# Layer-norm roots by pairs of row tiles on ScalarE, sums ahead of statistics, and banks closed to early maxima ahead of transposes and products

## The chip, the cores and the metric

The kernel runs on one core of a Trainium2 chip. The core has five engines with queues of their own: TensorE (PE, matrix products into PSUM banks), VectorE (DVE), ScalarE (ACT), GpSimd (POOL) and SyncE (SP, which mostly issues DMA transfers). An engine executes its queue in the order in which the program was written, and waits at an instruction until the semaphores it needs are set. The metric is device microseconds of one execution; lower is better.

## The reference

Two kinds of layers alternate, twice each, on `x` of 2048 rows by 512 columns in float32:

```python
x = x + fnet(layernorm(x))     # Re(DFT over rows (DFT over columns))
x = x + attention(layernorm(x))
x = x + fnet(layernorm(x))
x = x + attention(layernorm(x))

def layernorm(x, eps=1e-5):
    m, v = mean(x), var(x)                  # of each row
    return (x - m) / sqrt(v + eps)

def attention(x):                           # 32 query heads of 16 columns, one key and value head
    q, k, v = heads(x @ wq), x @ wk, x @ wv
    p = softmax(q @ k.T * 16 ** -0.5)
    return merge(p @ v) @ wo
```

## The kernel before

The kernel calls the same code twice (`L` is 0 and 1), once for each pair of a Fourier layer and an attention layer. In each, phase A computes the Fourier layer, and, as rows come out of it, the layer norm, keys, values and queries of the attention; phase B computes the attention. In layer 0 phase A lasts from 0 to about 655 us and in layer 1 from about 1800 to 2440 us. The change touches phase A only.

Phase A goes through 128 steps `n`, 32 for each block `tb` of four row tiles of 128 rows. The steps multiply normalized rows with the sequence DFT matrix into four banks `z[d]`, as three products of high and low parts (`ch`, `cl` of the matrix, `xnh`, `xnl` of the rows). From step 48 on (`ROWS`) this is done by `z_rows` (L749) in pairs of 64-row matmuls for two steps at once. The banks of z are in the two pairs named `x` in PSUM. The second half of such a group waits for a relay (L542): ScalarE copies two elements of `xnl` onto themselves, which orders the halves.

When a block's steps are done, its y rows follow (`y_tile` for block 0, `y_rows`, L555, for blocks 1 and 2): the column DFT. `y_out` then, for each row tile, adds the residual (`x1`, L537) on VectorE, stores the sum to `mid` by a DMA from GpSimd, and takes the layer-norm statistics (`ln_stats`, L136 and L137, into `mv`). `prep_tasks` spreads the rest of the block's attention input over the next block's first steps. The table `ts` there maps (step within the block, z quarter done) to tasks; a key without a quarter is the end of that step:

- `ln_root(t0, 4)`: variance plus epsilon on VectorE (L142, `lnv`), its square root on ScalarE (L143, `lnw`), for all four tiles at once; `ln_inv`: a reciprocal on VectorE (L148) and one Newton round in four small GpSimd operations (L149 to L152), into `rs`.
- `ap(j)`: subtract the mean and multiply with the inverse root, on VectorE (`ln_apply`, L183).
- `tr(j)`: transpose a row tile by four matmuls with the identity (L258) into the single bank `z`, and split it into high and low parts (ScalarE L82, L83, GpSimd L84).
- `do_kv`: keys and values of the block, twelve matmuls (L87 to L89) into a bank `y`, of which there are three; `kv_lo` (L286) and `k_diff` (L296, L297, L300) read that bank on VectorE and ScalarE; `v_tr` (L305, L306) transposes the values through bank `z`.
- `q_mm`, four times: queries, each twelve matmuls into a bank `y`, then stores.

Into all this the kernel mixes "early maxima". Phase B needs the maximum of each query row's scores; the table `EARLY` lists those that phase A already computes, with the steps of load, start and deadline. One maximum is one score matmul (L440) into a free `y` or `z` bank and a reduce on VectorE (L454, into `mxp` or `mxe`); where keys come as differences (`kd`), ScalarE and a fused VectorE operation (L444, L449) do it in two parts. When and into which bank a maximum goes is fixed while the program is written, by a small clock model: `clk` holds an estimated time for TensorE, VectorE, ScalarE and each bank, `spend` and `held` advance it, `pump` places a maximum wherever the model says that a bank is free, and `flush(n)` places in a row whatever has passed its deadline at step `n`. The DFT matrix's splits for later steps (`c_split`: a cast on ScalarE, L78, and a difference on GpSimd, L79) come two steps ahead, for two steps at once.

Of the kernel before, what the change touches and what calls it, by code (L numbers as in the profile page):

```python
# [17 lines left out]
P = 128  # L18
# [8 lines left out]
EPS = 1e-5  # L27
# [20 lines left out]
def fnet_mqa_kernel(ctx: ExitStack, tc: tile.TileContext, x_in, ct, dt_, wq, wkv, wo, out):  # L48
# [48 lines left out]
    nc.gpsimd.memset(v1[:, :, DH:DH + 1], 1.0)  # L97
    kone = sb.tile([P, 1], F32, name="kone")
# [40 lines left out]
    def ln_root(t0, n):  # L139
        v = sb.tile([P, 4], F32, name="lnv", bufs=2)[:, :n]  # L140
        w = sb.tile([P, 4], F32, name="lnw", bufs=2)[:, :n]
        nc.vector.tensor_scalar(v, mv[:, t0:t0 + n, 1], EPS, None, op0=ALU.add)  # L142
        nc.scalar.activation(w, v, AF.Sqrt)  # L143
        return t0, n, v, w
# [43 lines left out]
    def make_layer(L, src, mid, dst, last):  # L188
# [75 lines left out]

        def kv(t0, n, xth, xtl, vt=None, now=True):
            pk = bank("y")[:, :n * P]
            spend(pe=2.9, act=1.2)
            held("y", clk["pe"] + 2.5)
# [39 lines left out]
        def q_mm(tb, g, xth, xtl):  # L308
            wh, wl = st["wqh", g]
            pq = bank("y")  # L310
            spend(pe=2.9, act=1.2)
            held("y", clk["act"])
# [100 lines left out]
        st["skew"], st["rel"] = 0, {}  # L413
# [9 lines left out]
        def issue(e, pr, part, g, force):  # L423
            i, kb = EARLY[e][:2]
            tag = "z" if clk["z"] <= clk["y"][0] else "y"
# [5 lines left out]
            if free > clk["pe"] + 0.05 and not force:  # L431
                return False
# [6 lines left out]
            pm = bank(tag)  # L439
            nc.tensor.matmul(pm, o.qT[i][gs, pr, :], k[gs, c0:c0 + 512], start=True, stop=True)  # L440
# [94 lines left out]
        def y_out(t, y, x1):  # L535
            spend(dve=1.3)
            nc.vector.tensor_add(x1, y, x1)  # L537
            nc.gpsimd.dma_start(mid[t], x1)
            ln_stats(x1, t)
# [4 lines left out]
        def y_rows(tb, pairs, zh, zl, x1, after):  # L544
            ys = [pair() for _ in pairs]
            at = 0
            for h in range(2):
                for w, y in zip(pairs, ys):
# [15 lines left out]
                    else:  # L564
                        for e in range(2):
                            y_out(4 * tb + w[e], y[:, e, :], x1[w[e]])
# [71 lines left out]
        def prep_tasks(tb, x1):  # L638
# [3 lines left out]
            def alloc():  # L642
                st["root"] = ln_root(4 * tb, 4)
# [13 lines left out]
            ts[0] = [alloc]  # L657
            ts[1, 1] = [lambda: ln_inv(*st["root"])]
            ts[2, 0], ts[2, 2] = [ap(0)], [ap(1)]
            ts[2] = [lambda: tr(0)]  # L660
            ts[3, 0], ts[3, 2] = [ap(2)], [ap(3)]
            ts[3] = [lambda: tr(1)]
            ts[4, 1] = [lambda: tr(2)]
# [527 lines left out]
```

## Time and profile before

| what | us |
|---|---|
| median of three runs (lowest, highest) | 3596.87 (3596.85, 3599.12) |
| the profiled execution | 3599.28 |
| span of its trace | 3597.4 |
| TensorE busy | 3513.1 |
| VectorE busy | 2685.1 |
| ScalarE busy | 2504.9 |
| GpSimd busy | 897.0 |

In the profile, a group is named by its line, engine and operation, and by out<-in in the program's tile names. Rows of the timeline give start, duration, engine, line, operation and tiles; in brackets stands how long the engine was idle just before, and which instruction ended that. Rows of the waits give the waiting line, the line waited for, the total, how often, and the longest. Rows of windows give for each stretch its length, the busy times and instruction counts of PE, PEld (weight loads), DVE, ACT and POOL, then TensorE's granted clock (1.00 is full), the DMA share and GB/s. The y rows of block 1 end at about 282 us in layer 0, and those of block 2 at about 460; in layer 1 the same places are at about 2064 and 2242.

### The profile page before, as it was taken

What the parts mean: (1) busy time and instruction counts of PE and PEld (TensorE: products, weight loads), DVE (VectorE), ACT (ScalarE), POOL (GpSimd) and SP (SyncE); (2) the same over time, 40 slices, a digit from 0 to 9 for tenths busy, and PEclk for the clock granted to TensorE, in tenths of its full rate; (3) what the DMA queues carried; (4) which work ended last, traced back from release to release, by engine and by line L of the source; (5) the groups of instructions that cost most, each with busy time, mean ns of one, the idle gap of its engine ahead of it and who ended that gap; (6) DMA issues with size and microseconds to landing.
All of it is one profiled execution on the core that took longest, in us unless ns stands there. A gap on an engine that the chain in (4) does not pass through costs nothing.

```text
span 3597.4 us, 64452 instructions
## 1 busy us (share of the span) xinstructions
PE 3513.1 (98%) x24672; PEld 1891.4 (53%) x24672; DVE 2685.1 (75%) x4853; ACT 2504.9 (70%) x3204; POOL 897.0 (25%) x1284
## 2 busy tenths in 40 slices
PE   8999999899999999999999999999999999999999
PEld 6797878433333333333378878783333333333333
DVE  6166776788888888888511777758888888888883
ACT  3322734688888888888933237437888888888888
POOL 5543332221122112212254342422010110011011
PEclk9999999999999999999999999999999999999999
DMA  6544252311111101110143342422111111111110
GB/s 185 158 152 128 97 162 69 104 42 43 34 35 46 39 22 25 46 37 25 40 132 115 128 142 88 155 79 81 51 34 34 42 44 34 25 32 40 34 25 25
DMA packets 224899, 254.55 MB, mean 71 GB/s; under 512 B 52880, under 2 KB 174800, under 8 KB 217424
## 3 DMA queue, kind: packets, MB, share of 16 engines
q1 hardware_dynamic: 210384, 233.12, 21.3%
q0 software_dynamic: 14208, 17.33, 1.8%
q8 instruction: 194, 3.18, 0.4%
q14 instruction: 113, 0.93, 0.1%
HBM read 184.02 MB, written 65.27 MB: 69 GB/s over the span
## 4 chain that ended last, share of the span: by engine, by line
PE 87%; DVE 4%; issue 3%; ACT 3%; DMA 2%; POOL 1%; SPq 0%; ACTq 0%; POOLq 0%; DVEq 0%
PE z L930 28%; PE x L916 19%; PE y L389 13%; PE x L749 10%; PE y L87 2%; PE x L555 2%; PE y L440 2%; PE y L89 2%; PE y L88 2%; PE x L89 1%; PE x L87 1%; PE x L88 1%; DVE mxe L454 1%; DVE mxp L454 1%; PE z L440 1%
## 5 line engine op out<-in xcount | busy, mean ns | idle before, releaser
L919 ACT ACTIVATE slot<-x 128x1024 f32<-128x1024 f32 x2000 | 1945.9, 1024 | 293.3 <-PE x L916 279.1
L390 DVE TENSOR_REDUCE mxp<-y 128x1 f32<-128x512 f32 (+1 forms) x3008 | 1872.7, 678 | 200.7 <-PE y L389 182.0
L930 PE MATMUL z<-slot,v 128*32 128x512 f32 x8192 | 1097.5, 606 | 1.5 <-DVE row L934 0.7
L916 PE MATMUL x<-slot,kz 64*128 64x512 f32 x2976 | 681.0, 451 | 8.3 <-DMA slot<-mt 5.3
L916 PEld LDWEIGHTS x<-slot,kz 64*128 64x128 f32 x2976 | 280.9, 184 | 753.0 <-ACT slot L919 685.8
L389 PE MATMUL y<-kz,slot 64*128 64x512 f32 (+1 forms) x2240 | 598.3, 394 | 5.4 <-DVE kz L286 3.0
L79 POOL TENSOR_TENSOR cl<-craw,ch 128x512 fp32r<-128x512 f32 x236 | 302.5, 1299 | 253.7 <-ACT ch L78 228.1
L930 PEld LDWEIGHTS z<-slot,v 128*32 128x32 f32 x8192 | 163.5, 108 | 363.3 <-issue 332.9
L749 PE MATMUL x<-cl,xnh 64*128 64x512 f32 (+1 forms) x1536 | 354.5, 354 | 0.0
L749 PE MATMUL x<-ch,xnh 64*128 64x512 f32 (+1 forms) x1536 | 342.5, 359 | 9.0 <-ACT row L82 5.3
L749 PE MATMUL x<-ch,xnl 64*128 64x512 f32 (+1 forms) x1536 | 347.5, 359 | 0.0
L389 PEld LDWEIGHTS y<-kz,slot 64*128 64x128 f32 x2240 | 288.2, 187 | 29.8 <-DVE mxp L390 11.4
L508 POOL DMA_DIRECT2D slot<-mt x224 | 111.0, 503 | 616.4 <-PE y L389 481.0
L78 ACT CAST ch<-craw 128x512 fp32r<-128x512 f32 x256 | 152.7, 619 | 133.1 <-PE x L749 55.0
L440 PE MATMUL y<-kz,slot 64*128 64x512 f32 x602 | 233.5, 399 | 2.0 <-DVE kraw L296 1.0
L749 PEld LDWEIGHTS x<-ch,xnh 64*128 64x128 f32 x1536 | 213.8, 185 | 27.7 <-ACT row L82 9.1
L749 PEld LDWEIGHTS x<-cl,xnh 64*128 64x128 f32 x1536 | 220.8, 185 | 7.6
L749 PEld LDWEIGHTS x<-ch,xnl 64*128 64x128 f32 x1536 | 216.3, 185 | 12.8 <-issue 4.8
L971 POOL TENSOR_TENSOR row<-row,row 128x256 f32<-128x256 f32 x63 | 46.4, 737 | 678.2 <-DMA row<-rd 654.1
L454 DVE TENSOR_REDUCE mxe<-y 128x1 f32<-128x512 f32 x310 | 194.9, 678 | 14.2 <-PE y L440 14.0
L87 PE MATMUL x<-ch,xnh 128*128 128x512 f32 x384 | 155.6, 405 | 14.2 <-ACT ch L78 10.8
L88 PE MATMUL x<-cl,xnh 128*128 128x512 f32 x384 | 154.3, 402 | 3.4 <-POOL cl L79 2.8
(190 smaller groups left out, 4080.2 us busy)
## 6 DMA issues: line engine op xcount, KB each, us to landing
craw<-ct_in SPq DMA_DIRECT2D x112, 512.0 KB
slot<-qd SPq DMA_DIRECT2D x44, 1024.0 KB
qd<-row SPq DMA_DIRECT2D x144, 128.0 KB
od<-row SPq DMA_DIRECT2D x252, 64.0 KB
row<-wqd SPq DMA_DIRECT2D x48, 256.0 KB
row<-x_in SPq DMA_DIRECT2D x32, 256.0 KB
mid<-row POOLq DMA_DIRECT2D x32, 256.0 KB, 2.4
craw<-ct_in SPq DMA_DIRECT2D x32, 256.0 KB
```

What stands on the lines that cost most here:

```text
L78: nc.scalar.copy(hi, raw)
L79: (eng or nc.vector).tensor_sub(lo, raw, f(hi))
L87: nc.tensor.matmul(ps_, ah, bh, start=start, stop=False)
L88: nc.tensor.matmul(ps_, ah, bl, start=False, stop=False)
L389: nc.tensor.matmul(pm, o.qT[i][gs, pr, :], kz[gs, c0:c0 + n], start=True, stop=True)
L390: nc.vector.reduce_max(to, pm, axis=AX.X)
L440: nc.tensor.matmul(pm, o.qT[i][gs, pr, :], k[gs, c0:c0 + 512], start=True, stop=True)
L454: nc.vector.reduce_max(to, pm, axis=AX.X)
L749: nc.tensor.matmul(z[d], a[gs, s, d * P:(d + 1) * P], b[gs, :], start=first and q < 2 and e == 0, stop=last and q > 1 and e == len(turns) - 1)
L916: nc.tensor.matmul(st["e"][:, g, :], kz[64 * g:64 * g + KR, c * P:(c + 1) * P], o.qT[i][64 * g:64 * g + KR, cp:cp + 4, :], start=True, sto ...
L919: nc.scalar.activation(ptiles[i, s_][:, 2 * w:2 * w + 2, :], st.pop("e"), AF.Exp, scale=DH ** -0.5)
L930: nc.tensor.matmul(a[32 * j:32 * j + 32, :], v1[:, c, :], pt[:, j, :], start=c == 0, stop=c == NT - 1)
```

## The change

1. `ln_root` no longer adds epsilon on VectorE ahead of the root. ScalarE takes the root of the variance in `mv` directly, with epsilon from a small tile `eps` as its bias; variance plus epsilon, which the Newton round needs, is made on GpSimd.
2. Roots go by pairs of row tiles, issued right behind the statistics of each pair, instead of once for four. The first pair's `ln_inv` stands right behind the y rows.
3. In `y_rows`, both tiles' residual sums stand ahead of both tiles' statistics.
4. In `prep_tasks` the applies, transposes, kv and q products, with the loads and stores that go with them, stand about one step sooner. `hold` closes bank `z` to maxima ahead of each transpose. `keep` allocates the `y` bank of a product some quarters ahead and lets at most two maxima into the other two until the product.
5. In `EARLY` some loads and starts move by about one step.

On ScalarE, from the relays in block 1's y rows of layer 0 into the next block. Before (`slot` relays belong to the y rows, `xnl` relays to z; `ch<-craw` are the casts of the DFT matrix, `lnw` is the root):

```order
L542 CAST slot_2384<-slot_2384 128x2 x2
L78 CAST ch<-craw 128x512 x2
L542 CAST xnl<-xnl 128x2 x2
L143 ACTIVATE lnw<-lnv 128x4
L78 CAST ch<-craw 128x512 x2
L542 CAST xnl<-xnl 128x2 x2
L82 ACTIVATE row_2794<-z 128x512
```

After:

```order
L561 CAST slot_2395<-slot_2395 128x2 x2
L144 ACTIVATE lnw<-mv,eps 128x2 x2
L78 CAST ch<-craw 128x512 x2
L561 CAST xnl<-xnl 128x2 x2
L82 ACTIVATE row_2756<-z 128x512
L83 CAST slot_2707<-row_2756 128x4x128
```

The two roots now stand ahead of the casts, and so ahead of the first two `xnl` relays of the new block.

On VectorE, from the second pair's statistics at the same place to the subtractions behind kv. Before:

```order
L142 TENSOR_SCALAR lnv<-mv 128x4
L148 RECIPROCAL rs<-lnw 128x4
L183 TENSOR_SCALAR row_2145<-row_2145,mv,rs 128x512
L454 TENSOR_REDUCE mxp_2766<-z 128x1
L454 TENSOR_REDUCE mxp_2766<-y 128x1 x2
L183 TENSOR_SCALAR row_2147<-row_2147,mv,rs 128x512
L454 TENSOR_REDUCE mxp_2766<-y 128x1
L454 TENSOR_REDUCE mxp_2766<-z 128x1
L454 TENSOR_REDUCE mxp_2766<-y 128x1 x2
L183 TENSOR_SCALAR row_2149<-row_2149,mv,rs 128x512
```

After:

```order
L150 RECIPROCAL rs<-lnw 128x2
L185 TENSOR_SCALAR row_2156<-row_2156,mv,rs 128x512
L150 RECIPROCAL rs<-lnw 128x2
L185 TENSOR_SCALAR row_2158<-row_2158,mv,rs 128x512
L185 TENSOR_SCALAR row_2160<-row_2160,mv,rs 128x512
L185 TENSOR_SCALAR row_2162<-row_2162,mv,rs 128x512
L470 TENSOR_REDUCE mxp_2807<-y 128x1 x13
L470 TENSOR_REDUCE mxp_2807<-z 128x1
```

The epsilon operation is gone, and the four applies stand in a row ahead of the reduces; the first thirteen maxima behind them are all in `y` banks.

On TensorE, the flush of overdue maxima ahead of step 95, in block 2 of layer 0 (`x2` rows are two such matmuls). Before:

```order
L440 MATMUL y<-kz,slot_3516 128x512
L440 MATMUL y<-kd,slot_3516 128x512 x2
L440 MATMUL z<-kz,slot_3516 128x512
L440 MATMUL y<-kz,slot_3516 128x512
L440 MATMUL y<-kd,slot_3516 128x512 x2
L440 MATMUL z<-kz,slot_3516 128x512
L440 MATMUL y<-kz,slot_3516 128x512
```

After:

```order
L456 MATMUL z<-kz,slot_3485 128x512
L456 MATMUL y<-kd,slot_3485 128x512 x2
L456 MATMUL y<-kz,slot_3485 128x512
L456 MATMUL z<-kz,slot_3485 128x512
L456 MATMUL y<-kd,slot_3485 128x512 x2
L456 MATMUL y<-kz,slot_3485 128x512
L456 MATMUL z<-kz,slot_3485 128x512
L456 MATMUL y<-kd,slot_3485 128x512 x2
L456 MATMUL y<-kz,slot_3485 128x512
L456 MATMUL z<-kz,slot_3485 128x512
L456 MATMUL y<-kd,slot_3485 128x512 x2
L456 MATMUL y<-kz,slot_3485 128x512
```

One further maximum like the first row follows, so that 17 stand in a row without a z matmul between them, where there were 9. Behind the kv product of block 1, three maxima were placed ahead of the transposes of the values before; now, past the same three, four more in `y` banks follow ahead of them, and the last of these four takes the bank that kv had. The reduce of the first of the four stands ahead of kv's subtractions on VectorE.

The diff:

```diff
@@ -33,10 +33,10 @@
 
 
 EARLY = [
-    (1, 0, 2, 44, 48, 63, 16), (2, 0, 3, 44, 48, 63, 16), (3, 0, 8, 45, 48, 66, 16), (0, 0, 0, 64, 66.5, 79, 16),
-    (0, 1, 0, None, 71.5, 79, 16), (3, 1, 8, None, 71.5, 84, 16), (4, "f", 2, 77, 79.5, 95, 16), (5, "f", 3, 77, 79.5, 95, 16),
-    (6, "f", 8, 84, 87, 128, 16), (2, 1, 0, 96, 98, 111, 16), (1, 1, 1, 96, 98, 111, 16), (1, 2, 1, None, 103.5, 111, 8),
-    (7, "f", 2, 107, 109.5, 119, 16), (0, 2, 8, 101, 103.5, 128, 16),
+    (1, 0, 2, 43, 48, 63, 16), (2, 0, 3, 43, 48, 63, 16), (3, 0, 8, 44, 48, 66, 16), (0, 0, 0, 64, 66.5, 79, 16),
+    (0, 1, 0, None, 70.3, 79, 16), (3, 1, 8, None, 70.3, 84, 16), (4, "f", 2, 76, 78.5, 95, 16), (5, "f", 3, 76, 78.5, 95, 16),
+    (6, "f", 8, 84, 87, 128, 16), (2, 1, 0, 96, 98, 111, 16), (1, 1, 1, 96, 98, 111, 16), (1, 2, 1, None, 102.3, 111, 8),
+    (7, "f", 2, 106, 108.5, 119, 16), (0, 2, 8, 101, 103.5, 128, 16),
 ]
 ROWS = 48
 KEPT = [e for e in EARLY if e[0]]
@@ -95,6 +95,8 @@
     v1 = sb.tile([P, NT, 32], F32, name="v1")
     nc.gpsimd.memset(v1, 0.0)
     nc.gpsimd.memset(v1[:, :, DH:DH + 1], 1.0)
+    eps = sb.tile([P, 1], F32, name="eps")
+    nc.gpsimd.memset(eps, EPS)
     kone = sb.tile([P, 1], F32, name="kone")
     kmask = sb.tile([P, 1], F32, name="kmask")
     t_ = sb.tile([P, 1], F32, name="ktmp")
@@ -139,8 +141,8 @@
     def ln_root(t0, n):
         v = sb.tile([P, 4], F32, name="lnv", bufs=2)[:, :n]
         w = sb.tile([P, 4], F32, name="lnw", bufs=2)[:, :n]
-        nc.vector.tensor_scalar(v, mv[:, t0:t0 + n, 1], EPS, None, op0=ALU.add)
-        nc.scalar.activation(w, v, AF.Sqrt)
+        nc.scalar.activation(w, mv[:, t0:t0 + n, 1], AF.Sqrt, bias=eps)
+        nc.gpsimd.tensor_scalar(v, mv[:, t0:t0 + n, 1], EPS, None, op0=ALU.add)
         return t0, n, v, w
 
     def ln_inv(t0, n, v, w):
@@ -262,10 +264,19 @@
             else:
                 split_ps(v[0], xth, xtl)
 
+        def keep(after):
+            st["pk"], st["kept"] = bank("y"), 3
+            held("y", clk["pe"] + 1.4 + 2.8 + after)
+
+        def kept():
+            st["kept"] = 0
+            return st["pk"]
+
         def kv(t0, n, xth, xtl, vt=None, now=True):
-            pk = bank("y")[:, :n * P]
+            pk = (bank("y") if now else kept())[:, :n * P]
             spend(pe=2.9, act=1.2)
-            held("y", clk["pe"] + 2.5)
+            if now:
+                held("y", clk["pe"] + 2.5)
             for k in range(NK):
                 mm3(pk, wkvh[:, k, :], wkvl[:, k, :], xth[:, k, :n * P], xtl[:, k, :n * P], k == 0, k == NK - 1)
             cs = slice(t0 * P, (t0 + n) * P)
@@ -307,9 +318,8 @@
 
         def q_mm(tb, g, xth, xtl):
             wh, wl = st["wqh", g]
-            pq = bank("y")
+            pq = kept()
             spend(pe=2.9, act=1.2)
-            held("y", clk["act"])
             for k in range(NK):
                 ks = slice(k * P, (k + 1) * P)
                 mm3(pq, wh[:, ks], wl[:, ks], xth[:, k, :], xtl[:, k, :], k == 0, k == NK - 1)
@@ -410,7 +420,8 @@
 
         work = {e: [(pr, part, g) for pr in range(ent[6]) for part in ("db" if ent[1] == "f" else "u") for g in range(2)]
                 for e, ent in enumerate(EARLY)}
-        st["skew"], st["rel"] = 0, {}
+        st["skew"], st["rel"], st["hold"] = 0, {}, False
+        roots = {}
 
         def pump(n, only=None):
             for e in sorted((e for e in work if work[e] and EARLY[e][4] <= n), key=lambda e: EARLY[e][5]):
@@ -422,13 +433,15 @@
 
         def issue(e, pr, part, g, force):
             i, kb = EARLY[e][:2]
-            tag = "z" if clk["z"] <= clk["y"][0] else "y"
+            tag = "z" if clk["z"] <= clk["y"][0] and not st["hold"] else "y"
             free = clk["z"] if tag == "z" else clk["y"][0]
             if part == "b":
                 free = max(free, st["rel"][g][1] - 0.7)
             elif part == "d" and g in st["rel"]:
                 return False
             if free > clk["pe"] + 0.05 and not force:
+                return False
+            if tag == "y" and st.get("kept") == 1:
                 return False
             if "mxe" not in st:
                 st["mxe"] = sb.tile([P, len(KEPT), NPAIR, 2], F32, name="mxe")
@@ -437,6 +450,9 @@
             gs = slice(64 * g, 64 * g + KR)
             k, c0 = (st["kd"], 0) if part == "d" else (kz, 512 if part == "b" else 512 * kb)
             pm = bank(tag)
+            if tag == "y" and st.get("kept"):
+                st["kept"] -= 1
+                assert st["kept"]
             nc.tensor.matmul(pm, o.qT[i][gs, pr, :], k[gs, c0:c0 + 512], start=True, stop=True)
             ready = max(clk["pe"], free) + 0.5
             if part == "d":
@@ -533,10 +549,13 @@
             y_out(t, y, x1)
 
         def y_out(t, y, x1):
-            spend(dve=1.3)
+            y_add(t, y, x1)
+            ln_stats(x1, t)
+
+        def y_add(t, y, x1):
+            spend(dve=1.5)
             nc.vector.tensor_add(x1, y, x1)
             nc.gpsimd.dma_start(mid[t], x1)
-            ln_stats(x1, t)
 
         def relay(ap):
             nc.scalar.copy(ap, f(ap))
@@ -563,7 +582,11 @@
                         relay(zl[1][:, NK - 1, w[0] * P:(w[0] + 2) * P].rearrange("p (a b) -> p a b", a=2)[:, :, :1])
                     else:
                         for e in range(2):
-                            y_out(4 * tb + w[e], y[:, e, :], x1[w[e]])
+                            y_add(4 * tb + w[e], y[:, e, :], x1[w[e]])
+                        for e in range(2):
+                            ln_stats(x1[w[e]], 4 * tb + w[e])
+                        if tb < 3:
+                            roots[w[0]] = ln_root(4 * tb + w[0], 2)
 
         def a_start():
             if L:
@@ -640,7 +663,6 @@
             ts = {}
 
             def alloc():
-                st["root"] = ln_root(4 * tb, 4)
                 st["xt"] = [slot(2 + j, F32R).rearrange("p (k t) -> p k t", k=NK) for j in range(2)]
 
             def tr(tt):
@@ -654,24 +676,38 @@
             def ap(j):
                 return lambda: (spend(dve=0.8), ln_apply(x1[j], x1[j], 4 * tb + j))
 
-            ts[0] = [alloc]
-            ts[1, 1] = [lambda: ln_inv(*st["root"])]
-            ts[2, 0], ts[2, 2] = [ap(0)], [ap(1)]
-            ts[2] = [lambda: tr(0)]
-            ts[3, 0], ts[3, 2] = [ap(2)], [ap(3)]
-            ts[3] = [lambda: tr(1)]
-            ts[4, 1] = [lambda: tr(2)]
-            ts[4] = [lambda: tr(3), lambda: [wq_load(g) for g in range(2)]]
-            ts[6, 0] = [do_kv]
-            ts[6, 3] = [lambda: (kv_lo(4 * tb, 4), k_diff(tb) if tb < 2 else None)]
-            ts[6] = [lambda: v_tr(4 * tb, 4, st["vt"])]
+            def hold():
+                st["hold"] = True
+
+            def tr_(tt):
+                st["hold"] = False
+                tr(tt)
+
+            ts[0, 0] = [alloc]
+            ts[0, 2] = [ap(0)]
+            ts[0, 3] = [lambda: ln_inv(*roots[2])]
+            ts[0] = [ap(1)]
+            ts[1, 0] = [hold]
+            ts[1, 2] = [lambda: tr_(0), ap(2)]
+            ts[1] = [ap(3)]
+            ts[1, 3] = [hold]
+            ts[2, 1] = [lambda: tr_(1)]
+            ts[2, 2] = [hold]
+            ts[3, 0] = [lambda: tr_(2)]
+            ts[3, 1] = [hold]
+            ts[3, 3] = [lambda: tr_(3), lambda: [wq_load(g) for g in range(2)]]
+            ts[4, 2] = [lambda: keep(2.6)]
+            ts[5, 0] = [do_kv]
+            ts[5, 3] = [lambda: (kv_lo(4 * tb, 4), k_diff(tb) if tb < 2 else None), hold]
+            ts[6, 1] = [lambda: (st.update(hold=False), v_tr(4 * tb, 4, st["vt"]))]
             for g in range(4):
-                ts[7 + g] = [lambda g=g: q_mm(tb, g, *st["xt"])]
+                ts[6 + g, 1] = ts.get((6 + g, 1), []) + [lambda: keep(0.9)]
+                ts[6 + g] = [lambda g=g: q_mm(tb, g, *st["xt"])]
                 if g < 2:
-                    ts[7 + g].append(lambda g=g: wq_load(g + 2))
+                    ts[6 + g].append(lambda g=g: wq_load(g + 2))
                 if g:
-                    ts[7 + g].append(lambda g=g: q_store(tb, g - 1))
-            ts[11] = [lambda: q_store(tb, 3)]
+                    ts[6 + g].append(lambda g=g: q_store(tb, g - 1))
+            ts[10] = [lambda: q_store(tb, 3)]
             return {(base + k[0], k[1]) if isinstance(k, tuple) else base + k: v for k, v in ts.items()}
 
         def phase_a(extra):
@@ -844,8 +880,11 @@
                     if n < ROWS:
                         for tt in range(4):
                             y_tile(tb, tt, zh, zl, x1[tt])
+                            if tt % 2:
+                                roots[tt - 1] = ln_root(4 * tb + tt - 1, 2)
                     else:
                         y_rows(tb, ((0, 1), (2, 3)), zh, zl, x1, {})
+                    ln_inv(*roots[0])
                     for k, v in prep_tasks(tb, dict(x1)).items():
                         for fn in v:
                             if isinstance(k, tuple):
```

## Prediction

> **What bounds the kernel now.** I read the page's first part, then its chain that ended last:
>
> ```profile
> PE 3513.1 (98%) x24672; PEld 1891.4 (53%) x24672; DVE 2685.1 (75%) x4853; ACT 2504.9 (70%) x3204; POOL 897.0 (25%) x1284
> PE 87%; DVE 4%; issue 3%; ACT 3%; DMA 2%; POOL 1%; SPq 0%; ACTq 0%; POOLq 0%; DVEq 0%
> ```
>
> TensorE carries the chain. The change removes none of its matmuls, so it can pay only where TensorE stands still in the two layers' Fourier phases. The list of TensorE's waits (total, times, longest) has these at the spots the change touches:
>
> ```profile
> PE z L258 <- DVE mxp L454: 6.7, 6, 2.0
> PE z L258 <- DVE mxe L454: 5.4, 6, 1.4
> PE x L749 <- DVE row L537: 3.7, 4, 0.9
> PE y L87 <- DVE mxe L454: 2.8, 6, 0.5
> PE y L87 <- DVE mxp L454: 1.9, 4, 0.5
> PE z L440 <- DMA slot<-qd: 1.1, 2, 0.8
> PE y L440 <- DVE kraw L296: 1.0, 2, 0.5
> PE z L440 <- ACT v L306: 0.5, 2, 0.3
> ```
>
> Sum: 6.7+5.4+3.7+2.8+1.9+1.1+1.0+0.5 = 23.1 us. The timeline places the largest; the bracket is idle before, and who ended it:
>
> ```profile
> 284.30 0.50 PE L749 MATMUL x<-ch,xnh 64*128 64x512 f32 x2 [0.92 <-DVE row L537]
> 294.26 0.86 PE L258 MATMUL z<-ident,row 128*128 128x128 f32 x4 [2.00 <-DVE mxp L454]
> 472.30 0.66 PE L258 MATMUL z<-ident,row 128*128 128x128 f32 x4 [1.40 <-DVE mxe L454]
> 2076.42 1.11 PE L258 MATMUL z<-ident,row 128*128 128x128 f32 x4 [2.00 <-DVE mxp L454]
> ```
>
> The windows view adds a second price. After the busy times of five engines comes the granted clock:
>
> ```profile
> 291.20:294.60 3.40, 1.40 (x12) 0.86 (x9) 3.00 (x6) 0.20 (x1) 0.71 (x1) 1.00 0.50 146
> 294.60:298.00 3.40, 3.40 (x17) 2.48 (x17) 1.70 (x3) 1.22 (x2) 1.27 (x1) 0.50 0.32 86
> 298.00:301.40 3.40, 3.40 (x28) 2.51 (x28) 2.98 (x6) 0.60 (x2) 0.00 (x0) 1.00 0.00 0
> ...
> 2076.30:2079.70 3.40, 3.28 (x14) 2.52 (x16) 1.04 (x3) 1.22 (x2) 0.81 (x1) 0.51 0.43 129
> ```
>
> Right after each 2.00 us stall TensorE ran 3.4 us at half clock: 17 and 14 matmuls where a full window holds 28, so 1.3 to 1.7 us lost, 1.5 each. Two windows are 3.0 us. A full window also prices one matmul: 3.40/28 = 0.12 us; a pair of 64-row matmuls is 0.24.
>
> **The change, part by part.** Block means 32 steps; "start" is the end of a block's y rows, 281.98 here. The rows on VectorE, GpSimd and ScalarE behind it:
>
> ```profile
> 282.01 0.69 DVE L537 TENSOR_TENSOR row<-x,row 128x512 f32<-128x512 f32 x1 [2.27 <-PE x L555]
> 283.57 0.67 DVE L537 TENSOR_TENSOR row<-x,row 128x512 f32<-128x512 f32 x1
> 285.01 0.18 DVE L137 BATCH_NORM_AGGREGATE mv<-bst 128x2 f32<-128x6 f32 x1
> 285.22 2.44 DVE L142 TENSOR_SCALAR lnv<-mv 128x4 f32<-128x4 f32 x1
> 289.27 1.49 DVE L183 TENSOR_SCALAR row<-row,mv,rs 128x512 f32<-128x512 f32 x1 [1.15 <-POOL rs L152]
> 297.51 0.54 DVE L183 TENSOR_SCALAR row<-row,mv,rs 128x512 f32<-128x512 f32 x1
> ```
> ```profile
> 285.09 2.54 POOL L79 TENSOR_TENSOR cl<-craw,ch 128x512 fp32r<-128x512 f32 x2
> 289.04 0.20 POOL L152 TENSOR_TENSOR rs<-rs,lnw 128x4 f32<-128x4 f32 x1
> 289.19 2.73 POOL L79 TENSOR_TENSOR cl<-craw,ch 128x512 fp32r<-128x512 f32 x2
> ```
> ```profile
> 271.24 1.14 ACT L78 CAST ch<-craw 128x512 fp32r<-128x512 f32 x2
> 283.41 0.20 ACT L542 CAST xnl<-xnl 128x2 fp32r<-128x2 f32 x1 [11.04 <-PE x L749]
> 286.01 0.20 ACT L542 CAST xnl<-xnl 128x2 fp32r<-128x2 f32 x1 [2.40 <-PE x L749]
> 287.70 0.20 ACT L143 ACTIVATE lnw<-lnv 128x4 f32<-128x4 f32 x1 [1.50 <-DVE lnv L142]
> ```
>
> *Both sums, then statistics.* The second add ends at 282.01+0.69+0.69 = 283.39 instead of 284.24, just when TensorE asks (284.30−0.92 = 283.38). All four waits go: −3.7.
>
> *Maxima held off the z bank, layer norm applies ahead of maxima.* The twelve L258 waits are for the reduce of a maximum that took the one z bank. None is placed there any more in those stretches, so 12.1 us go, and both half-clock windows with them: −3.0. By the Trainium skill ("TensorE: Matmul & The Clock Gate", Why this matters for your kernels) only PE-idle gaps of more than about 3 us drop the clock. The trace differs: 2.00 us did. By that rule the windows have another cause, stay, and the sum is 3.0 smaller.
>
> *Reserved y banks.* The L87 waits go: −4.7. *Loads and starts of maxima a step sooner.* The query rows that were late (1.1) are asked for one step earlier against the same start: −1.1. The kraw and v rows (1.0, 0.5) are replaced by what stands under kv: −1.5. The q stores and wq loads stand one step earlier on SP, with the products they belong to; that queue shows no other wait at these spots: 0. In block 0, whose y rows are whole-row matmuls, the transposes move too, with few maxima near them: 0.
>
> *Roots.* L142's 2.44 us on VectorE goes; its work costs GpSimd one op of 0.20 (row 289.04) per pair, ahead of L79 whose splits are two steps early: 0. In layer 0's first tiles ScalarE is 0.2 sooner and GpSimd 0.3 later: 0, between −0.7 and +0.7.
>
> *What the roots' new place costs.* For ScalarE's two relays (L542, L561 after) the second half of the block's first z matmuls waits. They stood behind casts that had run at 271.24, and ahead of the root. Now the order is root of rows 2 and 3, the two casts, the relays. Statistics of row 3 end at 285.01+0.18 = 285.19, as before; root 0.11 to 0.2 (a small ScalarE op lets the next start 0.11 later: a 0.20 relay precedes the casts of 271.24), casts 1.14, relay 0.20: 286.6 to 286.7. TensorE asks after the six pairs that the 283.38 gap held back. They took from 284.30 to 285.9 (relay row 286.01), so it asks at 283.38+1.6 = 285.0, or 284.8 by 0.24 a pair. Stall 1.2 to 1.9; I take 1.5. Blocks 1 and 2, both layers: 4×1.5 = **+6.0**.
>
> *kv.* Rows of the product's surroundings:
>
> ```profile
> 317.42 1.39 DVE L286 TENSOR_TENSOR kz<-y,kz 16x512 fp32r<-16x512 f32 x2
> 318.83 0.69 DVE L296 TENSOR_TENSOR kraw<-kraw,y 128x512 f32<-128x512 f32 x1
> 323.52 0.68 DVE L454 TENSOR_REDUCE mxp<-z 128x1 f32<-128x512 f32 x1
> ```
> ```profile
> 319.55 0.72 ACT L297 ACTIVATE kd<-kraw,kmask 128x512 fp32r<-128x512 f32 x1 [1.74 <-DVE kraw L296]
> 320.30 0.21 ACT L306 COPY v<-z 128x64 f32<-128x64 f32 x1
> ```
>
> After the change the reduce of a fourth maximum stands on VectorE ahead of the three subtractions that free kv's bank, and TensorE has three more maxima close behind that fourth. With K the end of kv, TensorE reaches the fourth at K+2.5 (nine pairs, three maxima); its reduce ends near K+3.7. The sixth, which wants its bank, is due at K+3.2: 0.5. The seventh, which wants kv's bank, is due 0.6 after that, at K+4.3, and gets it at K+3.7+1.39+0.69 = K+5.8: 1.5. The v copy on ScalarE stands behind kd (0.72), two casts (1.14) and a relay (0.20): K+8.0, against a maximum on z due about K+7: 0.5 to 1.0, I take 0.6. Block 1: 2.6. Block 2 has no kraw subtraction: 0.5+0.7 = 1.2. Two layers: 2×3.8 = **+7.6**, between 4 and 9.
>
> *Forced maxima.* Ahead of step 95 the order had 9 maxima in a row; now 17, since they were held back before.
>
> ```profile
> 423.25 0.40 PE L440 MATMUL y<-kz,slot 64*128 64x512 f32 x1
> 424.73 0.50 PE L440 MATMUL y<-kz,slot 64*128 64x512 f32 x1
> 426.23 0.49 PE L440 MATMUL y<-kz,slot 64*128 64x512 f32 x1 [0.20 <-ACT rel L444]
> ```
>
> The pattern repeats every four: 1.49/4 = 0.37 each, against 0.12 between z matmuls. 8×(0.37−0.12) = 2.0 per layer: **+4.0** (2 to 5).
>
> *VectorE's lag.* The removed stalls let VectorE catch up. Now four applies stand ahead of thirteen reduces, each between 0.54 (GpSimd idle) and 1.49 (beside L79). At 1.49 the last ends some 9 us after the statistics, 0.7 to 1.8 later than the fourth maximum asks for a bank; at 0.54 in time. Before, no L440 waited for a reduce of this kind, so I take 0.5 at four places: **+2.0** (0 to 7).
>
> Sum: −23.1−3.0+6.0+7.6+4.0+2.0 = −6.5 on the profiled 3599.28, or 3592.8. The median of the runs lies 2.4 lower (3596.87): 3590.4, rounded **3590**.
>
> **Rivals.** 0.2%, about what a measurement of this kernel tells from no change, is 7.2 us: 3589.7 and 3604.1 are the bounds.
> - *Half clock moves along.* The new relay stalls (1.5) lie between 1.40, which kept full clock, and 2.00, which lost it; the kv stalls of block 1 come close together too. Four windows and two: 6×1.5 = +9 on 3590: 3599; with the relays alone 3596. For it: the relay stall's upper bound 1.9. Against: 1.40 did not.
> - *New stalls are smaller.* If casts and root wait for less than I read, or later maxima sit where the bank is free, relay and kv give back half or all of 13.6: 3577 to 3584. For it: my times are of the old schedule.
> - *Slower: the applies wait for GpSimd as L142 did.* L142 began at 285.22 beside L79 (285.09) and ended at 287.66, when both L79 had ended: it was locked out of two in a row. Four applies now stand between L79 and L84 work with every reduce behind them. At 2.44 instead of 1.49 each, 3.8 later per block, TensorE short of banks by as much at four places: +15, so 3605. It decides from 3.5 a place, a mean apply of 2.4. By the Trainium skill ("SBUF — State Buffer", SBUF: two separate sides) the port pair of VectorE and GpSimd is an exclusive lock and the loser fully blocks; the trace agrees (2.44 and 1.49).
> - *The windows stay.* By the clock rule named above: 3593. The two windows begin right behind the two 2.00 us stalls and behind no shorter one shown, which speaks against it.
>
> **How the numbers follow.** Forecast 0.50 (its own range 3585 to 3595, so half of it faster by over 0.2%), half clock 0.17, smaller stalls 0.16, applies locked 0.12 (0.1 of it past 3604), windows stay 0.05. Of half clock I count 0.04 past 3604 with lag on top. Faster 0.25+0.16 = 0.41; slower 0.10+0.04 = 0.14; same the rest, 0.45. Range 3579 to 3603: it leaves out the best of the smaller stalls and the worst of the lock.
>
> **What would show it.** Right: no L258 wait on a reduce, no L749 wait on an add, full clock around the first transposes; new waits of z matmuls on the xnl relay (1.2 to 1.9, four times), of maxima on kraw, kz and v behind kv, 17 maxima in a row in about 6 us. Wrong: relay stalls near zero, applies past 2 us, or half-clock windows behind the relays.

## The result, and the profile after

The changed kernel is slower. Its median is 3608.79 us (3605.87 to 3612.87, seven runs) against 3596.87 us (3593.57 to 3599.76, seven runs) of the kernel before: a ratio of 1.0031, 95% interval 1.0022 to 1.0041. The profiled execution's span is 3606.8 us, 9.4 longer than that of before; the traces thus show 9.4 of the 11.9 us by which the medians differ.

The page's first part shows no less work on TensorE. The same 24672 matmuls take longer (3526.9 us busy instead of 3513.1):

```profile
PE 3526.9 (98%) x24672; PEld 1885.1 (52%) x24672; DVE 2688.9 (75%) x4842; ACT 2506.2 (69%) x3210; POOL 911.5 (25%) x1332
```

The waits of TensorE in the changed kernel that answer to those of the prediction (L785 is L749 of before, L260 is L258, L456 is L440):

```profile
PE x L785 <- ACT xnl L561: 5.6, 4, 1.4
PE y L456 <- DVE mxe L470: 4.4, 2, 2.2
PE z L260 <- DVE row L185: 4.0, 3, 1.6
PE y L456 <- DVE kraw L307: 2.5, 2, 1.3
PE z L260 <- DVE mxp L470: 1.6, 2, 0.8
PE z L456 <- DVE mxe L470: 1.2, 2, 0.6
PE y L456 <- DVE kz L297: 1.1, 2, 0.6
PE z L456 <- ACT v L317: 0.3, 1, 0.3
```

Without the third row they sum to 16.7 us, where before there were 23.1: 6.4 less. (Of the third row, 3.2 belong to the phase's tail, where before there were 4.0, and 0.80 to a transpose of block 0 at 154.33, which is new.) Over all of TensorE's waits in the span the change gains 5.2 us (72.7 instead of 77.9). Those on the sums, on the query rows' load and, but for 0.2 us, on maxima ahead of products are gone, and those of transposes on reduces fell from 12.1 to 1.6.

What turned the gain around is time that counts as busy: 13.8 us more of it, for the same matmuls. A good part of this is the clock. The windows view, at the places where the granted clock fell in the steps of phase A that are worked in half-row matmuls:

```profile
423.10:426.50 3.40, 3.40 (x10) 1.67 (x12) 2.81 (x9) 2.51 (x5) 0.00 (x0) 0.51 0.00 0
426.50:429.90 3.40, 3.40 (x18) 2.65 (x20) 2.17 (x7) 1.61 (x3) 0.00 (x0) 0.50 0.00 0
474.00:477.40 3.40, 3.29 (x13) 2.33 (x15) 2.30 (x5) 1.22 (x2) 0.85 (x2) 0.55 0.18 28
2098.60:2102.00 3.40, 3.40 (x19) 2.33 (x17) 3.12 (x4) 1.53 (x5) 2.56 (x2) 0.57 0.00 0
2102.00:2105.40 3.40, 3.40 (x11) 2.18 (x8) 1.77 (x3) 0.19 (x1) 0.39 (x1) 0.50 0.00 0
2211.60:2215.00 3.40, 3.40 (x16) 2.41 (x18) 2.05 (x7) 2.39 (x4) 0.00 (x0) 0.52 0.00 0
2259.90:2263.30 3.40, 3.40 (x13) 2.33 (x15) 2.12 (x4) 1.22 (x2) 0.67 (x2) 0.50 0.16 19
2263.30:2266.70 3.40, 3.40 (x19) 2.41 (x15) 2.35 (x5) 0.19 (x1) 1.07 (x1) 0.55 0.15 58
```

In these steps that makes eight windows of 3.4 us at half clock instead of two. Elsewhere in the span there are eight, where there were ten. So the whole trace has four more, up to 1.7 us each, 7 us at most (less where TensorE waits anyway); the mean granted clock fell from 0.994 to 0.992 (0.991 to 0.993 in all seven executions). The eight lie at the flush of forced maxima (three), behind kv in layer 1 (two), and behind the 2.2 us wait of block 2 (three). The rest of the busy time is in part the maxima of the flush, which run with nothing beside them; not all of it was placed.

Since every z matmul is in both traces, the delay can be read at the same matmul. Change of the delay in each stretch, after minus before:

```
stretch                                      layer 0   layer 1
y rows of block 1 to the flush at step 95      -4.4      -2.2
the flush and block 2's y rows                 +4.5      +3.9
the rest of block 2 (first transposes)         +1.5      +3.0
```

Block 1 gains, as forecast; the flush and block 2 lose more. The rest of the 9.4 is 0.8 at the start and smaller amounts elsewhere, in phase B too.

### The profile page after: what moved, and what is told of

It reads as the page before. It is cut to its first block, busy times and chain, and to the rows that moved or that the text cites. A ratio compares the mean times of both kernels' runs of the same rounds, so it can differ in the third digit from the quotient of the medians.

```text
span 3606.8 us, 64507 instructions
## 1 busy us (share of the span) xinstructions
PE 3526.9 (98%) x24672; PEld 1885.1 (52%) x24672; DVE 2688.9 (75%) x4842; ACT 2506.2 (69%) x3210; POOL 911.5 (25%) x1332
## 5 line engine op out<-in xcount | busy, mean ns | idle before, releaser
L79 POOL TENSOR_TENSOR cl<-craw,ch 128x512 fp32r<-128x512 f32 x236 | 304.5, 1308 | 285.5 <-ACT ch L78 226.9
L785 PE MATMUL x<-cl,xnh 64*128 64x512 f32 (+1 forms) x1536 | 355.7, 356 | 0.0
L785 PE MATMUL x<-ch,xnl 64*128 64x512 f32 (+1 forms) x1536 | 348.0, 361 | 5.6 <-ACT xnl L561 5.6
L785 PE MATMUL x<-ch,xnh 64*128 64x512 f32 (+1 forms) x1536 | 346.6, 360 | 4.5 <-ACT row L82 4.4
L456 PE MATMUL y<-kz,slot 64*128 64x512 f32 x614 | 242.5, 407 | 8.9 <-DVE mxe L470 4.4
L785 PEld LDWEIGHTS x<-ch,xnh 64*128 64x128 f32 x1536 | 214.4, 186 | 25.9 <-ACT row L82 8.3
L785 PEld LDWEIGHTS x<-ch,xnl 64*128 64x128 f32 x1536 | 214.7, 186 | 24.4 <-ACT xnl L561 8.0
L785 PEld LDWEIGHTS x<-cl,xnh 64*128 64x128 f32 x1536 | 218.7, 186 | 10.2
```

Source lines behind the costliest of these rows:

```text
L79: (eng or nc.vector).tensor_sub(lo, raw, f(hi))
L785: nc.tensor.matmul(z[d], a[gs, s, d * P:(d + 1) * P], b[gs, :], start=first and q < 2 and e == 0, stop=last and q > 1 and e == len(turns) - 1)
```

## The experiments

All ratios are against runs of the kernel before on the same chip, with 95% intervals; the changed kernel stands at 1.0031 on that scale. 0.001 is 3.6 us.

**The relay's place.** In the changed kernel, the second pair's root behind the first `xnl` relay:

```diff
-                        if tb < 3:
-                            roots[w[0]] = ln_root(4 * tb + w[0], 2)
+                        if tb < 3 and w[0] == 0:
+                            roots[0] = ln_root(4 * tb, 2)
...
+            ts[0, 1] = [root2]          # ln_root(4 * tb + 2, 2) for blocks 1 and 2
```

> The changed kernel, with the root of a block's second pair issued after the first xnl relay instead of ahead of the casts (blocks 1 and 2). If the relay's place behind root and casts costs what its four waits show (1.4 us each), those four waits vanish and the time falls by 5 to 6 us against the changed kernel, to about 3603. If the stall only holds back a VectorE that is late anyway, the waits vanish but come back at the first transposes or maxima behind them, and the time stays within 2 us of 3609.

Measured: 3611.17 us, 1.0036 (1.0023 to 1.0048), no gain. The four relay waits are gone, but these two groups of the trace grew by 3.2 and 3.0 us:

```profile
PE y L456 <- DVE mxe L470: 7.6, 2, 3.8
PE z L260 <- DVE row L185: 7.0, 7, 2.3
```

So the relay stall was real and sized right, and this way of removing it gained nothing. In block 2 VectorE was late behind it anyway (the next run shows why). In block 1 the edit itself made VectorE later: the third and fourth apply took 2.92 us there, where they had taken 1.00. What the stall alone is worth is therefore not shown.

**The store that reads the row.** In the changed kernel the applies write to another row tile (and the transposes' copy takes the old one):

```diff
-                return lambda: (spend(dve=0.8), ln_apply(x1[j], x1[j], 4 * tb + j))
+                def fn():
+                    spend(dve=0.8)
+                    xn[j] = half(4 + j)
+                    ln_apply(xn[j], x1[j], 4 * tb + j)
+                return fn
```

> The changed kernel, with the layer norm applies writing to another row tile, so that they need not wait for the store of the sum (mid) that still reads the old one. If the store holds VectorE in block 2, the idle 2.3 us ahead of the third apply vanishes in both layers, with it the 2.2 us wait of the fourth maximum and the half clock behind it: 6 to 10 us less than the changed kernel, about 3601. If VectorE is late there because four applies stand ahead of the reduces beside GpSimd's work, the 2.2 us wait stays above 1.5 and the time within 2 us of 3609.

Measured: 3602.67 us, 1.0009 (1.0000 to 1.0018): 8 us less than the changed kernel, as expected of the store. The changed kernel's VectorE in block 2 shows what went (start, duration, what ended the idle time before):

```profile
465.99 1.48 DVE L185 TENSOR_SCALAR row<-row,mv,rs 128x512 f32<-128x512 f32 x1 [1.28 <-POOL rs L154]
467.46 1.43 DVE L185 TENSOR_SCALAR row<-row,mv,rs 128x512 f32<-128x512 f32 x1
471.22 2.24 DVE L185 TENSOR_SCALAR row<-row,mv,rs 128x512 f32<-128x512 f32 x2 [2.32 <-DMA mid<-row]
473.38 2.47 DVE L470 TENSOR_REDUCE mxe<-y 128x1 f32<-128x512 f32 x4
```
```profile
474.11 0.60 PE L456 MATMUL y<-kz,slot 64*128 64x512 f32 x1 [2.22 <-DVE mxe L470]
```

The third apply waits 2.32 us for the DMA that stores the same row, and all reduces queue behind it; TensorE's fourth maximum finds no bank until 474.11 (2.22 us), and the clock falls. Around it the DMA engines are full, and the stores take long:

```profile
464.00:467.00 3.00, 1.60 (x16) 0.99 (x14) 1.69 (x4) 1.51 (x5) 2.00 (x6) 1.00 1.00 374
DMA to landing us min/median/max: 2.4/5.5/8.8
```

In that 464 to 467 window the last three numbers are full clock, DMA engines busy all the time and 374 GB/s: the queries' load of that step (`slot<-qd`, issued at 461.75) goes on beside the stores. The second row is the landing time of this block's four stores: the first two took 2.4 and 2.7 us, the last two, issued behind that load, 8.4 and 8.8. Before, it was much the same (2.4, 2.4, 9.2 and 8.4). In the run with the other tile, the third and fourth apply take 0.55 and 0.54 and no maximum waits there for a reduce in a `y` bank.

**The reserved banks.** The changed kernel without `keep`:

```diff
-            ts[4, 2] = [lambda: keep(2.6)]
...
-                ts[6 + g, 1] = ts.get((6 + g, 1), []) + [lambda: keep(0.9)]
...
-            pq = kept()
+            pq = bank("y")
```

> The changed kernel without the banks reserved ahead of kv and q products (they are allocated at the product, as before); 7 maxima in a row ahead of step 95 instead of 17. If the reserved banks hold the maxima back until they are forced, the two stretches at step 95 give back what they lost (4.5 and 3.9 us) and 0.5 to 1 more, and the half clock there goes, while the waits of the products on maxima come back (4.7): net 3 to 6 us less, about 3604. If the flush is long because the block has fewer stalls to hide maxima in, the stretches stay as long and only the products' waits are added: 3611 to 3614.

Measured: 3606.05 us, 1.0018 (1.0009 to 1.0027), 5 us less. Where the changed kernel lost 4.5 and 3.9 us at the flush, this run gains 0.7 and 0.4 against before: the reserved banks are the cause of the long flush. Much of that is lost again elsewhere: the waits of products on maxima came back (6.3 us), block 1 of layer 0 gains 0.3 us against before instead of 4.4, and in block 2 the wait on `mxe` grew to 3.5.

**The three together, and two of them.**

> The three edits together. If their causes are separate, the gains add: 15 to 20 us less than the changed kernel, 3589 to 3594, so faster than the kernel before by 3 to 8 us. If one stall hides another, it stays above 3597.

Measured: 3603.80 us, 1.0017 (1.0008 to 1.0026), only 5 us less than the changed kernel instead of the expected 15 to 20. Block 2 still waited 2.6 us for a reduce. VectorE and GpSimd there:

```profile
466.13 1.42 DVE L185 TENSOR_SCALAR row<-row,mv,rs 128x512 f32<-128x512 f32 x1
468.65 2.88 DVE L185 TENSOR_SCALAR row<-row,mv,rs 128x512 f32<-128x512 f32 x2 [1.10 <-POOL rs L154]
```
```profile
468.57 1.28 POOL L84 TENSOR_TENSOR slot<-row,slot 128x512 fp32r<-128x512 f32 x1
469.80 2.85 POOL L79 TENSOR_TENSOR cl<-craw,ch 128x512 fp32r<-128x512 f32 x2
```

All four applies run beside GpSimd's wide operations and take 1.4 to 1.5 us each; with the relay's edit the last two do so as well. That gave the next two runs. First, the two edits without the relay's:

> Two of the three edits, other tile and no reserved banks, with the root where the change put it (7 maxima in a row ahead of step 95). If the relay edit is what spoils the three together, because it shifts the applies of rows 3 and 4 onto GpSimd's L84 and L79 (1.5 us each instead of 0.5), those applies take 0.5 here, no maximum waits over 1 us in block 2, and the time is about 13 us less than the changed kernel, at or just below the kernel before, 5 us less than with the three. If the applies are 1.5 here too, or the gain stays at 7, the relay edit is not the cause.

Measured: 3597.41 us, 1.0002 (0.9993 to 1.0011), 10 us less than the changed kernel. The third and fourth apply take 1.00 together, and the waits on `mxe` in `y` banks fall to 0.5 in all. So the edit that removed the relay's stall moved these applies onto GpSimd's work and cost some 5 us (3603.80 against 3597.41 on two chips; by the intervals of the two ratios between about 1 and 10).

**GpSimd's splits ahead of the Newton rounds.** The three edits (relay, other tile, no reserved banks), with both `ln_inv` of blocks 1 and 2 issued after the next steps' splits:

```diff
-                    ln_inv(*roots[0])
+                    if not tb:
+                        ln_inv(*roots[0])
...
+                    ln_inv(*roots[0])
                     roots[2] = ln_root(4 * tb + 2, 2)
+                    ln_inv(*roots[2])
```

> The three edits of the run before last in the list (relay, other tile, no reserved banks) and, in blocks 1 and 2, both pairs' reciprocals and Newton rounds moved behind the splits (L79) of the next two steps on GpSimd, so that no split runs while VectorE applies the layer norm. If the applies are late because GpSimd's splits lock them out (1.5 us and more each instead of 0.5), the four applies take about 0.5 each, the last ends 2 to 3 us sooner against the start of the block, and the wait of the fourth maximum in block 2 (2.6 us) falls below 0.5, against up to 1 us more at the first transpose: 4 to 8 us less than with the three edits, and no half clock at the first transposes. If the applies are late for another reason, their durations stay and the wait with them.

Measured: 3596.13 us, 0.9993 (0.9984 to 1.0003), 9 us less than the three alone. The applies run unhindered, and of the wait 0.3 a layer is left:

```profile
468.28 1.00 DVE L185 TENSOR_SCALAR row<-row,mv,rs 128x512 f32<-128x512 f32 x2 [2.28 <-POOL rs L154]
469.92 1.00 DVE L185 TENSOR_SCALAR row<-row,mv,rs 128x512 f32<-128x512 f32 x2 [0.64 <-POOL rs L154]
470.94 2.48 DVE L470 TENSOR_REDUCE mxe<-y 128x1 f32<-128x512 f32 x4
```

The price is 1.9 us more at the first transposes' waits for an apply (9.5 instead of 7.6), since the Newton rounds now come behind the splits. In this run L79 begins at 464.72, 0.13 into an L138 of 0.66 us, and an L139 of 0.18 us lies wholly inside it; both take no longer than elsewhere. It is the apply that is hindered.

**The bank that kv leaves.** Two tries on the stretch behind kv, both on top of the run with the Newton rounds moved (0.9993). First, kv's subtractions one z quarter sooner (`ts[5, 2]` instead of `ts[5, 3]`):

> The same, with kv's subtractions issued one z quarter sooner, ahead of the fourth maximum's reduce on VectorE. If the fourth maximum's reduce ahead of them makes kv's bank late, the waits on kraw and kz (1.0 and 0.3 each) fall below 0.3, and the half clock behind the kv product of block 1 goes: 2 to 6 us less than the run without it. If the half clock there has another cause, the clock drops there all the same.

Measured: 3598.94 us, 1.0004 (0.9994 to 1.0013). The waits rose instead of falling: on kraw from 1.0 to 1.9 and on kz from 0.3 to 1.2, although the bank was free 1.1 us sooner in layer 0 (315.03 against 316.13): the maximum that takes it asked 2.0 us sooner. So the order of the reduces does not decide this wait; when the clock model gives the bank out does. Next the model was told that the bank stays taken longer:

```diff
-            held("y", clk["pe"] + 2.5)
+            held("y", clk["pe"] + (4.6 if t0 < 12 else 2.5))
```

> The run with Newton rounds behind the splits, and with the clock model told that a kv bank stays taken for 4.6 us in blocks 0 to 2 instead of 2.5, which is about when VectorE frees it; 11 maxima in a row ahead of step 95 instead of 7. If the waits for kv's bank (kraw 1.0, kz 0.3) and the stretch at half clock behind the kv product of block 1 in layer 0 come from maxima placed into that bank too soon, the waits fall below 0.3, the half clock goes there, and the flush costs 1 us a layer more: 2 to 4 us less than the run without it. If that half clock has another cause, it stays and the time is 1 to 2 us more.

Measured: 3592.13 us, 0.9983 (0.9973 to 0.9992). The waits on kraw and kz are gone, but another stands in their place: a maximum in bank `z` waits 2.4 us for the copy of the values, in both layers, with the half clock behind it. The time is 4 us less than without the line by the ratios, as expected, but the two intervals overlap, so that gain is not shown.

**Parts alone on the kernel before.** Both sums ahead of both statistics, nothing else:

> The kernel before with one part of the change: both sums ahead of both statistics in the y rows. The four waits of z matmuls on the second add (0.9 us each) vanish. If they are worth what they show, 3 to 4 us less than before; if VectorE is late behind them anyway, the wait moves to the first transposes and the time stays within 1.5 us of before.

Measured: 3593.80 us, 0.9986 (0.9977 to 0.9995), and the trace's delay falls by 0.9 to 1.0 at each of the four places. This part alone is worth what its waits showed. With the root straight from the variance on top (four tiles at once):

> The kernel before with two parts: the sums ahead, and the root taken by ScalarE straight from the variance, for four tiles as before, with variance plus epsilon on GpSimd. If the 2.4 us that VectorE's epsilon operation was locked out is what made the first transposes late, their longest waits (2.0 and 1.4) and the half clock behind the 2.0 go in both layers: 8 to 14 us less than before. If the transposes wait for the maximum in their bank whatever comes ahead of it, these waits stay above 1 us and the gain is 3 to 5.

Measured: 3599.65 us, 1.0002 (0.9993 to 1.0012). The waits of the transposes stay:

```profile
PE z L260 <- DVE mxp L456: 6.7, 6, 2.0
PE z L260 <- DVE mxe L456: 4.7, 6, 1.1
```

So L142's 2.4 us was not what made them: they hang on the maximum in their bank. The first maxima also waited 1.70 and 1.23 us for the queries' rows in the two layers of this run, where they waited 0.36 and 0.78 before, with half clock behind it; that took 2.6 and 2.0 us in the two layers, more than the sums' gain there. Why these rows came later was not settled.

**The z bank closed, nothing moved.** The kernel before, with the sums ahead, and `hold` a quarter or half a step ahead of each transpose:

```diff
-            tag = "z" if clk["z"] <= clk["y"][0] else "y"
+            tag = "z" if clk["z"] <= clk["y"][0] and not st["hold"] else "y"
...
+            ts[2, 2] = ts.get((2, 2), []) + [hold]     # also at (3, 2), (4, 0), (4, 2)
```

> The kernel before with the sums ahead and with one more part: the z bank closed to maxima for half a step ahead of each transpose, transposes and products left at their old steps; 11 maxima in a row ahead of step 95 instead of 9. If the closed bank is what takes the transposes' waits away (12 us before, with 3 us of half clock), those on reduces fall to under 2 in total and the half clock behind the first transposes goes: 8 to 13 us less than with the sums alone. If VectorE is the one that is late, the waits move to maxima on y banks or to the applies, and the gain over the sums alone is under 4 us.

Measured: 3586.93 us, 0.9966 (0.9952 to 0.9980): faster than before by 0.34%, and by the ratios 7 us less than the sums alone, a little under the 8 to 13 expected. Of 12.1 us of waits on reduces ahead of transposes 2.6 are left. What stands out now, and what it does to the clock:

```profile
315.43 0.65 PE L440 MATMUL z<-kz,slot 64*128 64x512 f32 x1 [2.09 <-ACT v L306]
```
```profile
312.00:315.40 3.40, 1.34 (x12) 0.77 (x10) 2.55 (x5) 0.93 (x2) 0.00 (x0) 1.00 0.00 0
315.40:318.80 3.40, 3.37 (x16) 2.73 (x18) 3.36 (x6) 0.00 (x0) 0.00 (x0) 0.53 0.00 0
```

**The values' copy.** On top of it, the clock model holds bank `z` for 4 us behind block 1's values:

```diff
             nc.scalar.copy(v1[:, t0:t0 + n, :DH], pv_[:, :, DH:])
+            if t0 == 4:
+                clk["z"] = clk["pe"] + 4.0
```

> The run with the z bank closed ahead of transposes, and with the clock model told that this bank stays taken for 4 us behind the transposes of the values in block 1 (the one with kraw and kd ahead of the copy on ScalarE); 9 maxima in a row ahead of step 95, as before. If the 2.1 us that a maximum waited for the copy of the values in each layer, and the half clock behind it in layer 0, are worth what they show, 4 to 6 us less than that run, so 14 to 17 us less than before. If the maxima put off come back as waits elsewhere, within 2 us of that run.

Measured: 3587.29 us, 0.9960 (0.9947 to 0.9974), 0.40% less than its own runs of before. The run without this line had 0.9966 (0.9952 to 0.9980), so the expected 4 to 6 us are not shown. (That run's trace is of its slowest execution of five, 3591.6, so the two spans, 3589.7 and 3585.4, say little.) The wait on the copy is gone, but waits of products on `mxp` grew from 2.2 to 4.7 us, and 1.3 us on kraw came new: the maxima put off come back in part as waits elsewhere.

## Why the prediction was wrong

The forecast was 3590 (3579 to 3603); measured were 3608.8.

As a sum, the waits were forecast nearly right, partly by luck: 23.1 us going and 15.6 coming (relays, kv, VectorE's lag) make −7.5, and −6.4 was measured, with the forecast of kv 3.7 too large and that of VectorE's lag 2.4 too small. What failed is the rest: −3.0 for half clock and +4.0 for forced maxima make +1.0, and TensorE's busy time grew by 13.8.

- *Both sums, then statistics (−3.7)*: right. The waits vanished, and alone the part gave 5 us (2 to 8 by its interval).
- *Maxima held off the z bank (−12.1), y banks (−4.7), late rows (−1.1)*: right as waits: 1.6, 0.2 and none were left. A wait of 0.57 us on a reduce (205.97) came where the rows had been late. The transposes of block 0 had been put at 0; one of them now waits 0.80 us for its apply.
- *Relays (+6.0)*: 5.6 measured, with 1.4 a place. But taking them away, in the way tried, gave no time.
- *kv (+7.6)*: 3.9 as waits: 1.3 a layer for kraw in block 1, 0.6 for kz in block 2, 0.3 once for the values' copy. The sixth maximum did not wait.
- *Forced maxima (+4.0)*: right for the maxima themselves; what it left out is the clock. The 17 start 0.39 us apart from 420.06 to 426.28, against 0.37 taken. Across the row the delay grew by 3.2 and 2.8 us in the two layers; the eight further maxima would have cost some 1.0 among z matmuls elsewhere (8 times the forecast's 0.12), so about 2 a layer is their price, as forecast. But in so long a stretch of thin work the clock fell to a half, and the matmuls behind the row lost 1.7 and 1.3 us more. It is not the length alone: with 9 in a row the clock kept full before, and fell there in one layer in each of two later runs (at 428.83 with the root from the variance, at 2200.08 with the values' copy).
- *VectorE's lag (+2.0)*: the step that failed first. It was sized from applies of 0.54 and 1.49, at 0.5 a place; block 2's was 2.2, in both layers. The applies write in place on a row that a DMA is storing. Before, the third apply came at 474.86, and the store had landed at 470.62; moved to about 469 the apply was there first. The prediction looked at the DMAs that move with the steps (q stores, wq loads), and not at the one that reads the row. Giving the apply another tile took 8 us off.
- *Half clock (−3.0)*: the step that decided the sign. The two windows at the transposes went, and eight came elsewhere in these steps. The rival in which the half clock moves along was right in kind, and in its six further windows also in number; it had 0.17. It looked at the relays, where the clock stayed full at all four places, and at kv of block 1, where it fell in one layer; the rest came at the flush and at block 2's lag. By the waits (−5.2) and the forced maxima (some +4) alone the change would still have gained a little.
- *The rival of locked applies*: not 2.44 an apply, but 1.4 to 1.5 for two of four; no wait of the changed kernel hung on that alone. In the three edits together it did: moving GpSimd's splits out of the way gave 9 us. The Trainium skill ("SBUF — State Buffer", SBUF: two separate sides) has the two engines' port pair as an exclusive lock; the applies of 0.55 with GpSimd idle, 1.4 to 1.5 beside L79, and L142's 2.44 agree.
- *The clock rule*: the Trainium skill ("TensorE: Matmul & The Clock Gate", Why this matters for your kernels) has the clock fall after idle gaps of more than about 3 us. Here it fell behind 2.00, 2.09 and 2.22 us, and at the flush with no such gap at all.

Behind kv of block 1 the clock fell in layer 1 of the changed kernel and not in layer 0, with the same waits of 1.3 us; with the relay's edit it fell in layer 0 too (316.2 to 319.6). The traces narrow down why. In each trace the half-clock windows start whole multiples of 3.41 us apart (before, 294.58 and 2076.34 are 522 of them apart), so they lie on a fixed grid, and where it lies differs from trace to trace. Count the matmuls that start in each full-clock window of that grid, in the steps worked in half-row matmuls (one of 64 rows by 512 columns is 1, others by their size; half of these windows have 28 or more). Over all fourteen traces, each of the 32 windows with fewer than 11 was followed by half clock, none of the 2673 with more than 14, and 9 of the 43 in between. In layer 1 the wait behind kv lies whole in one window, and 10 start there; in layer 0 it runs past that window's end, 12 start, and the clock stayed. So a stall of this size costs half clock or not by where the grid falls on it. That is luck, which the prediction could not have worked out from the schedule.

## What to carry to other kernels

A stall on the bounding engine is worth its length only if what stands behind it is ready: look at the slowest other engine at that place before counting it, and at every DMA that still reads a buffer which a moved instruction writes. Work that is held back to keep a bank free comes back in a lump at its deadline, and a lump of thin work can cost clock as well. Here closing one bank a little earlier, with nothing else moved but the sums, gave more than the whole rearrangement: try the smallest part first.

## What the runs showed of the hardware that was not expected

- The granted clock halves in whole windows of 3.4 us on a fixed grid, here behind every window in which fewer than 11 half-row matmuls started (half of the windows have 28 or more) and behind none with more than 14. An idle gap is not needed: in the flush the page counts TensorE as busy, with one matmul of 0.39 us or more about every 0.37 to 0.41 us.
- An apply of 128x512 on VectorE takes 0.54 us, or 1.4 to 1.5 beside a GpSimd operation of the same size; bn_stats on the same rows took 0.66 with such an operation beginning 0.13 us behind it, and 0.66 to 0.70 without.
- A 256 KB store from GpSimd's queue landed in 2.4 us at best, and in 8.4 and 8.8 when issued behind a load of queries, with 374 GB/s in all.
